# Attention ahead of two feed-forward networks: plain float32 products on quarters and halves of TensorE's array in place of exact float32r halves

## The chip, the cores and the metric

One NeuronCore of one Trainium2 chip runs the whole program. The metric is the device time of one execution in microseconds; lower is better. A difference is judged by the median of several executions of both kernels on the same chip.

## What is computed

Attention over a sliding window of 64 positions, for 4 batches, 8 heads, 576 positions and a head size of 64. Its result, as 2304 rows of 512, goes through two networks: first the elementwise maximum of three products and an output product, then a product, a clipped square and another product.

```python
scores = np.matmul(q, k.transpose(0, 1, 3, 2)) / np.sqrt(64)
mask = (rel >= 0) & (rel < 64)                 # rel = query position - key position
attn = softmax(np.where(mask, scores, -1e9))   # sum + 1e-9 below the fraction
x = np.matmul(attn, v).transpose(0, 2, 1, 3).reshape(2304, 512)
h = np.maximum(np.maximum(x @ w1, x @ w2), x @ w3)   # w: 512 x 768
y = h @ w_out                                        # 768 x 512
h2 = y @ w_in                                        # 512 x 2048
g = np.where(h2 >= 1, h2, np.where(h2 <= -1, 0, (h2 + 1) ** 2 / 4))
out = g @ w_out2                                     # 2048 x 512
```

q, k and v are float32; the six weights are float64 in memory, 512 KB per tile.

## The kernel before

**Groups.** The 2304 positions are 36 groups of 64 positions, each with all 8 heads, as 4 pairs of heads: on the 128 partitions lie two heads of a pair, or 64 queries of each. Every group sees a window of 128 keys, its own 64 and the 64 ahead (64 keys for a batch's first group). Four groups make one block of 256 rows for the first network, of which there are nine.

**Exact halves.** A float32r product takes its operands at reduced precision. So the kernel splits each operand into a rounded high part and the rest (`sub` computes the rest), and adds three products, high by high, high by rest, rest by high. Weights, network inputs and, in this kernel, all attention operands are treated so. The networks stay as they are in the change.

**Stages of a group.** Each stage is a function, and the diff touches most of them:

- `load` and `vload` bring q, k and v. For the first 16 groups (`PET`) q and k come in natural layout, two groups on 128 partitions (`nat`); for later ones in pieces for VectorE's transposition (`raw`). v comes as keys by heads (`vr`).
- `prep` transposes q and k, for the first 16 groups on TensorE (`tp`, L234; one group is one half of the rows of `nat`), and writes q's halves, scaled, into a block-diagonal tile (`qbd`, ScalarE and L251) and k's halves into a ring of four groups (`kring`).
- `vprep` splits v (`vhl`, VectorE's L264 and a GpSimd subtraction).
- `qk` makes the scores `sps` (L287, L288; two products per pair), adds high and low parts and the mask (`t`, L292), then the negated scores and their minimum (`sm`, `nm`, L295).
- `ex` is the exponential (L306), `norm` the division (GpSimd, L317).
- `ptr` transposes the weights on TensorE (`pps`, L326) and splits them (`pthl`).
- `pv` multiplies them with v (`ops`, L339, L342; again two products per pair), adds the two parts (`xs`, `x`, L350) and splits the result into the network's input `xt`.

In what follows a score visit is a group's run of `sps` products on TensorE, a value visit its run of `ops` products.

**Weights.** `w_load` and `w_split` bring a float64 tile (`wst`) and turn it into a high and a rest part in `u`: three ScalarE operations, two VectorE ones (L156, L157), one on GpSimd. Four buffers hold tiles that wait for this. The first network has 24 such tiles, the second 32.

**Order.** The stages of the first four groups stand in an order written out by hand (`SEQ`). Those of the later ones get a due time by `STAGES`, relative to the items of the first network (`a_item`, L369, and `b_item`, L391). All is sorted by due time; then the framework's scheduler, which works with costs of its own, sets the order on each engine. Each engine runs its queue in order. All loads go through SyncE's queue.

**Buffers in PSUM.** `tp` and the networks' `ps` share three tiles of one bank (`pmm`); `sps` takes two banks, `pps` one, `ops` two.

## Time and profile before

| | us |
|---|---|
| median of 3 runs (875.35 to 876.76) | 876.25 |
| the profiled execution | 875.89 |
| its span, first to last instruction | 873.8 |
| TensorE busy with matmuls | 827.7 (95%) |
| VectorE busy | 497.1 (57%) |
| ScalarE busy | 419.9 (48%) |
| GpSimd busy | 202.0 (23%) |

Between the profiled execution's own time and its span lie 2.1 us of start and end. Rows of a timeline give the start, the duration, the engine, the line, the operation, the tiles it writes and reads, the used rows by columns of the array for a matmul, and how many merge in the row. Rows of a stretch give each engine's busy time with its number of instructions, the clock granted to TensorE (PEclk), the share of the DMA engines and GB/s. Rows of groups give the busy time, the mean duration in ns, and the idle time ahead.

### The profile page before, as it was taken

The page shows a single profiled execution, that of the slowest core. Times are in us where ns is not written, and L with a number is a line of the kernel's source. Part 1 is how long each engine was busy: PE and PEld are TensorE (multiplying, and loading weights), DVE is VectorE, ACT ScalarE, POOL GpSimd, SP SyncE. Part 2 cuts the span into 40 slices and gives each one's busy share as a digit, 9 for nine tenths or more (in the row PEclk, how much of TensorE's full clock was granted, in tenths as well). Part 3 has the DMA queues.
Part 4 walks back from the last instruction along what each step waited for, and adds up shares of the span by engine and source line. Part 5 has one row for each costly group of instructions (what it writes and reads, how often), then busy time and mean ns, then how long its engine had stood idle before and what let it go on. Part 6 is the DMA issues. An engine that isn't in the chain of part 4 may idle for free.

```text
span 873.8 us, 14317 instructions
## 1 busy us (share of the span) xinstructions
PE 827.7 (95%) x5264; PEld 743.7 (85%) x5264; DVE 497.1 (57%) x1216; ACT 419.9 (48%) x1043; POOL 202.0 (23%) x194
## 2 busy tenths in 40 slices
PE   5667899999999999999988999999999999999998
PEld 4567899999999999999877888888888888888897
DVE  5899975685858566645777833533343333333343
ACT  6997745564646475644778522322232223222232
POOL 3565642332323223333565300000000000000000
PEclk9998999999999999999999999999999999999999
DMA  9864534223414321202767100200010000100000
GB/s 235 195 167 145 153 65 89 65 52 66 80 45 72 109 62 43 79 20 68 229 222 248 60 1 1 74 11 1 1 48 25 1 1 12 49 1 1 24 25 25
DMA packets 128053, 62.66 MB, mean 72 GB/s; under 512 B 98288, under 2 KB 120816, under 8 KB 127984
## 3 DMA queue, kind: packets, MB, share of 16 engines
q1 hardware_dynamic: 127984, 61.76, 26.7%
q8 instruction: 41, 0.67, 0.3%
q14 instruction: 28, 0.23, 0.1%
HBM read 52.30 MB, written 9.44 MB: 71 GB/s over the span
## 4 chain that ended last, share of the span: by engine, by line
PE 79%; DVE 9%; DMA 5%; ACT 3%; issue 3%; POOL 1%; SPq 0%; DVEq 0%; ACTq 0%; POOLq 0%
PE acc L577 23%; PE hp L528 23%; PE ps L369 19%; PE ps L391 6%; DMA wst<-in_moe_w_in 3%; PE ops L339 2%; PE sps L287 2%; DVE wt L157 2%; DVE wt L156 2%; PE pps L326 1%; DMA wst<-in_moe_w_out 1%; POOL u L100 1%; PE sps L288 1%; PE ops L342 1%; DVE t L292 1%
## 5 line engine op out<-in xcount | busy, mean ns | idle before, releaser
L369 PE MATMUL ps<-xt,u 128*128 128x256 f32 x1944 | 246.7, 283 | 9.7 <-DVE ht L378 3.9
L369 PEld LDWEIGHTS ps<-xt,u 128*128 128x128 f32 x1944 | 235.1, 190 | 12.6 <-DVE ht L378 4.9
L557 ACT ACTIVATE u<-hp,half 128x512 f32<-128x512 f32 (+1 forms) x80 | 51.6, 645 | 253.8 <-PE hp L528 253.8
L528 PE MATMUL hp<-x2t,u 128*128 128x512 f32 (+1 forms) x720 | 161.6, 372 | 0.0
L577 PE MATMUL acc<-u,g 128*128 128x512 f32 x648 | 160.4, 396 | 0.0
L528 PEld LDWEIGHTS hp<-x2t,u 128*128 128x128 f32 x720 | 126.9, 188 | 27.2
L560 DVE SCALAR_TENSOR_TENSOR gt<-u,hp 128x512 f32<-128x512 f32 (+1 forms) x80 | 50.6, 632 | 166.7 <-ACT u L558 166.6
L577 PEld LDWEIGHTS acc<-u,g 128*128 128x128 f32 x648 | 121.0, 188 | 28.3
L391 PE MATMUL ps<-h,u 128*128 128x256 f32 x648 | 82.4, 284 | 4.6 <-ACT x2s L97 2.9
L391 PEld LDWEIGHTS ps<-h,u 128*128 128x128 f32 x648 | 78.5, 190 | 5.7 <-ACT x2s L97 3.1
L100 POOL TENSOR_TENSOR u<-wt,u 128x512 fp32r<-128x512 f32 x48 | 66.0, 1378 | 40.9 <-ACT u L97 40.8
L306 ACT ACTIVATE sm<-sm,nm 128x128 f32<-128x128 f32 (+1 forms) x144 | 55.3, 386 | 20.2 <-DVE nm L295 19.8
L317 POOL TENSOR_TENSOR sm<-sm,rs 128x512 f32<-128x512 f32 (+1 forms) x36 | 36.3, 1008 | 121.0 <-DVE rs L316 61.8
L564 DVE CAST g<-gt 128x512 fp32r<-128x512 f32 (+1 forms) x80 | 35.0, 437 | 45.6 <-PE acc L577 43.0
L100 POOL TENSOR_TENSOR vhl<-vr,vhl 128x512 fp32r<-128x512 f32 (+1 forms) x35 | 46.1, 1317 | 58.8 <-DVE vhl L264 24.8
L100 POOL TENSOR_TENSOR h<-ht,h 128x256 fp32r<-128x256 f32 x54 | 41.7, 773 | 65.2 <-ACT h L97 65.1
L157 DVE CUSTOM_DVE_ANT_0 wt<-wst,wt 128x1024 uint16<-128x1024 uint16 x56 | 54.2, 970 | 1.0
L528 PE MATMUL hp<-x2t,v 128*128 128x512 f32 (+1 forms) x240 | 54.4, 375 | 0.1
L287 PE MATMUL sps<-kring,qbd 128*128 128x256 f32 (+1 forms) x144 | 44.4, 377 | 10.4 <-DVE nm L295 8.4
L577 PE MATMUL acc<-v,g 128*128 128x512 f32 x216 | 53.6, 394 | 0.0
L100 DVE TENSOR_TENSOR g<-gt,g 128x512 fp32r<-128x512 f32 (+1 forms) x80 | 51.1, 639 | 2.6
L378 DVE TENSOR_TENSOR ht<-ps,ht 128x256 f32<-128x256 f32 x108 | 45.1, 418 | 10.6 <-PE ps L369 8.1
(68 smaller groups left out, 1067.2 us busy)
## 6 DMA issues: line engine op xcount, KB each, us to landing
wst<-in_moe_w_out SPq DMA_DIRECT2D x22, 512.0 KB, 4.3
wst<-in_moe_w SPq DMA_DIRECT2D x18, 512.0 KB, 4.1
wst<-in_moe_w_in SPq DMA_DIRECT2D x16, 512.0 KB, 4.1
vr<-in_v SPq DMA_DIRECT2D x24, 256.0 KB, 3.5
x_scratch<-x2s SPq DMA_DIRECT2D x36, 128.0 KB, 1.8
out<-ob SPq DMA_DIRECT2D x18, 256.0 KB, 2.0
x2r<-x_scratch SPq DMA_DIRECT2D x16, 256.0 KB, 2.8
vr<-in_v SPq DMA_DIRECT2D x19, 128.0 KB, 3.2
```

Source lines behind the costliest of these rows:

```text
L100: eng.tensor_tensor(dst, a, b, op=ALU.subtract)
L157: nc.vector.tensor_tensor(t, t, lo, op=ALU.add)
L287: nc.tensor.matmul(o[:, 0:2 * W], qh(p), win(p, slice(0, 2)), start=True, stop=False)
L306: nc.scalar.activation(sm[:, p, 0:W], sm[:, p, 0:W], AF.Exp, bias=d["nm"][:, p:p + 1], scale=-1.0, accum_out=ss[:, p:p + 1])
L317: nc.gpsimd.tensor_tensor(sm[:, :, 0:W], sm[:, :, 0:W], rs.unsqueeze(2).to_broadcast([P, NP, W]), op=ALU.mult)
L369: nc.tensor.matmul(ps[:, 0:n], w_col((w, f), wl, kt), xt[:, xl, kt, 0:n], start=(x == 0), stop=(x == len(passes) - 1))
L378: nc.vector.tensor_tensor(t[:, 0:n], ps[:, 0:n], part[j, f][:, 0:n], op=ALU.max)
L391: nc.tensor.matmul(ps[:, 0:n], w_col((3, f), wl, dt), hts[j, f][:, xl, 0:n], start=(x == 0), stop=(x == len(passes) - 1))
L528: nc.tensor.matmul(ps[:, 0:n], w_col((4, f), wl, kt), x2t[tb][:, xl, kt, 0:n], start=(x == 0), stop=(x == len(passes) - 1),)
L557: nc.scalar.activation(u[:, 0:n], ps[:, 0:n], AF.Relu, bias=half, scale=2.0 ** (-WS / 2 - 1))
L560: nc.vector.scalar_tensor_tensor(gt[:, 0:n], u[:, 0:n], 2.0 ** WS, ps[:, 0:n], op0=ALU.min, op1=ALU.max)
L577: nc.tensor.matmul(accs[t], g[:, gl, t * P:(t + 1) * P], wslot[5, f][:, wl * 512:(wl + 1) * 512], start=(f == 0 and x == 0), stop=(f == KF ...
```

## The change

The attention's operands are no longer split. Scores and values are plain float32 products.

- `prep`: for the first 16 groups, q and k of two groups are transposed at once, on the full array (L237), q copied to `qt2` by ScalarE, k to the ring by VectorE (L242). Later groups are transposed by VectorE straight to `qt` and the ring.
- `vprep` is gone; `pv` reads `vr`.
- `qk`: each head of a pair is a product of 64 rows by 64 columns of the array, the first head's on the upper left quarter, the second's on the lower right one (L272). `sps` is one bank, with two buffers. The scale of q has moved into L275, which now adds the mask itself.
- `ptr`: one copy in place of copy and rest.
- `pv`: each head is a product of its own on one half of the array's columns (L318), whose results lie where the network's input wants them; no sum of parts follows.
- `vr` has four buffers for two, `sm`, `nm`, `ss` and `rs` three for two. The hand order and the list of due times lose the entries of the stages that are gone.

```diff
-    "L0 V1 P0 P1 L2 V2 V3 v1 Q0 Q1 E0 N0 E1 N1 P2 T0 P3 Q2 v2 X0 T1 Q3 E2 N2 v3 E3 X1 N3 "
+    "L0 V1 P0 L2 V2 V3 Q0 Q1 E0 N0 E1 N1 P2 T0 Q2 X0 T1 Q3 E2 N2 E3 X1 N3 "
...
-    kring = apool.tile([P, NP, 2, 4, BL], F32R, name="kring")
-    qbd = [apool.tile([P, 2, NP, 2, BL], F32R, name=f"qbd{i}") for i in range(2)]
+    kring = apool.tile([P, NP, 4, BL], F32, name="kring")
...
     def prep(g):
         if g in pet:
-            tp = pmm.tile([P, 2, NP, BL], F32, tag="mm", name="tp")
-            r = slice(g % 2 * BL, g % 2 * BL + BL)
+            if g % 2:
+                return
+            qt = apool.tile([P, NP, 2, BL], F32, tag="qt2", name="qt2", bufs=2)
             for x in range(2):
+                tp = pmm.tile([P, NP, P], F32, tag="mm", name="tp")
                 for p in range(NP):
-                    nc.tensor.transpose(tp[:, x, p, :], nat[g // 2][r, x, p * P:(p + 1) * P], ident[r, r])
-            qt, kt = tp[:, 0], tp[:, 1]
+                    nc.tensor.transpose(tp[:, p, :], nat[g // 2][:, x, p * P:(p + 1) * P], ident)
+                tp = tp.rearrange("a p (t c) -> a p t c", t=2)
+                if x == 0:
+                    act_copy(qt, tp)
+                else:
+                    nc.vector.tensor_copy(kring[:, :, s:s + 2, :], tp)
...
-        qb = qbd[g % 2]
-        for h in range(2):
-            r = slice(h * BL, h * BL + BL)
-            act_copy(qb[r, 0, :, h, :], qt[r], scale=QSCALE)
-        act_copy(kring[:, :, 0, s, :], kt)
-        for h in range(2):
-            r = slice(h * BL, h * BL + BL)
-            nc.vector.scalar_tensor_tensor(
-                qb[r, 1, :, h, :], qt[r], QSCALE, f32(qb[r, 0, :, h, :]), op0=ALU.mult, op1=ALU.subtract
-            )
-        sub(nc.vector, kring[:, :, 1, s, :], kt, f32(kring[:, :, 0, s, :]))
...
     def qk(g):
-        sps = patt.tile([P, NP, 2, 2 * BL], F32, tag="s", name="sps")
+        sps = patt.tile([P, NP, 2 * BL], F32, tag="s", name="sps", bufs=2)
         for p in range(NP):
-            o = sps[:, p].rearrange("a b c -> a (b c)")
-            nc.tensor.matmul(o[:, 0:2 * W], qh(p), win(p, slice(0, 2)), start=True, stop=False)
-            nc.tensor.matmul(o[:, 0:W], ql(p), win(p, 0), start=False, stop=True)
-        t = apool.tile([P, NP, 2 * BL], F32, tag="t", name="t", bufs=1)
-        mb = mask.unsqueeze(1).to_broadcast([P, NP, W])
-        nc.vector.tensor_tensor(t[:, :, 0:W], sps[:, :, W:2 * W], mb, op=ALU.add)
+            for h in range(2):
+                r = slice(h * BL, h * BL + BL)
+                nc.tensor.matmul(sps[r, p, 0:W], d["q"][r, p, :], win(r, p), start=True, stop=True)
...
-                out=sm[:, p, 0:W], in0=sps[:, p, 0:W], in1=t[:, p, 0:W], scale=-1.0, scalar=BIG,
+                out=sm[:, p, 0:W], in0=sps[:, p, 0:W], in1=mask, scale=-QSCALE, scalar=BIG,
...
     def ptr(g):
-        act_copy(pt[0:W, :, 0, :], pps[0:W])
-        sub(nc.vector, pt[0:W, :, 1, :], pps[0:W], f32(pt[0:W, :, 0, :]))
+        act_copy(pt[0:W], pps[0:W])
...
     def pv(g, xt, off):
-        ops = patt.tile([P, NP, 2, P], F32, tag="o", name="ops")
+        ops = patt.tile([P, NP, BL], F32, tag="o", name="ops")
         for p in range(NP):
-            o = ops[:, p].rearrange("a b c -> a (b c)")
-            vc = slice(p * P, (p + 1) * P)
-            nc.tensor.matmul(
-                o, vh[0:W, 0, vc], pt[0:W, p].rearrange("a b c -> a (b c)"), start=True, stop=False
-            )
-            nc.tensor.matmul(o[:, 0:P], vh[0:W, 1, vc], pt[0:W, p, 0, :], start=False, stop=True)
-        for h in range(2):
-            r = slice(h * BL, h * BL + BL)
-            act_copy(xs[r], ops[r, :, 1, r])
-        for h in range(2):
-            r = slice(h * BL, h * BL + BL)
-            nc.vector.tensor_tensor(x[r], ops[r, :, 0, r], xs[r], op=ALU.add)
-        act_copy(xt[:, 0, :, off:off + BL], x)
-        sub(nc.vector, xt[:, 1, :, off:off + BL], x, f32(xt[:, 0, :, off:off + BL]))
+            for h in range(2):
+                r = slice(h * BL, h * BL + BL)
+                nc.tensor.matmul(ops[r, p, :], vr[0:W, 2 * p + h, :], pt[0:W, p, r], start=True, stop=True)
+        act_copy(xt[:, 0, :, off:off + BL], ops)
+        sub(nc.vector, xt[:, 1, :, off:off + BL], ops, f32(xt[:, 0, :, off:off + BL]))
```

**How it moves the order.** A row of an order is a line, an operation, the tile written and the tiles read, the shape, and how many follow each other. On TensorE, the start of the program before; the tiles are numbered here, `tp_133` being group 0, on the upper half of the rows, `tp_148` group 1, on the lower half, `tp_225` group 2:

```order
L234 MATMUL tp_133<-ident_85,nat_128 128x64 x4
L234 MATMUL tp_148<-ident_85,nat_128 128x64 x4
L234 MATMUL tp_133<-ident_85,nat_128 128x64 x4
L234 MATMUL tp_148<-ident_85,nat_128 128x64 x4
L234 MATMUL tp_225<-ident_85,nat_163 128x64 x4
```

And the start after, without numbers:

```order
L237 MATMUL tp<-ident,nat 128x128 x8
L272 MATMUL sps<-kring,qt_129 64x64 x8
L272 MATMUL sps<-kring,qt_129 64x128 x8
L237 MATMUL tp<-ident,nat 128x128 x8
L306 MATMUL pps<-ident,sm 64x128 x4
```

Sixteen transpositions on halves of the rows have become eight on the full array, and the scores of both groups follow each other.

On VectorE, the work from the first transpositions to the first scores before:

```order
L264 CAST vhl<-vr 128x512
L251 SCALAR_TENSOR_TENSOR qbd_102<-tp,qbd_102 64x4x64 x2
L100 TENSOR_TENSOR kring<-tp,kring 128x4x64
L251 SCALAR_TENSOR_TENSOR qbd_103<-tp,qbd_103 64x4x64 x2
L100 TENSOR_TENSOR kring<-tp,kring 128x4x64
L292 TENSOR_TENSOR t<-sps,maskA 128x4x64
L295 ISA sm,nm<-sps,t 128x64
```

And after:

```order
L242 COPY kring<-tp 128x4x128
L275 ISA sm,nm<-sps,maskA 128x64
```

One copy for two groups stands where eight operations stood ahead of the first scores' reduction.

On TensorE among the first network's products, a score visit before:

```order
L369 MATMUL ps<-xt,u_66 128x256 x12
L287 MATMUL sps<-kring,qbd_102 128x256
L288 MATMUL sps<-kring,qbd_102 128x128
L287 MATMUL sps<-kring,qbd_102 128x256
L288 MATMUL sps<-kring,qbd_102 128x128
L287 MATMUL sps<-kring,qbd_102 128x256
L288 MATMUL sps<-kring,qbd_102 128x128
L287 MATMUL sps<-kring,qbd_102 128x256
L288 MATMUL sps<-kring,qbd_102 128x128
L369 MATMUL ps<-xt,u_67 128x256 x12
```

And after, a score visit and a value visit:

```order
L337 MATMUL ps<-xt,u_70 128x256 x12
L272 MATMUL sps<-kring,qt_1095 64x128 x8
L337 MATMUL ps<-xt,u_71 128x256 x12
L318 MATMUL ops<-pt,vr 64x64 x8
L337 MATMUL ps<-xt,u_72 128x256 x12
```

Eight products on quarters or on halves stand where eight on the full array stood, between the same neighbours; they come and go by a change of the array's shape.

More of the change, by code (lines that the diff above doesn't have):

```diff
@@ L38 @@
 TAIL = 15
-STAGES = (-21, -9, -3, -2.5, 0, 0.2, 1, 6, 9)
+STAGES = (-21, -9, -3, 0, 0.2, 1, 6, 9)
 LP = -9
@@ L215, in vload @@
             return
-        t = apool.tile([P, H, D], F32, tag="vr", name="vr", bufs=2)
+        t = apool.tile([P, H, D], F32, tag="vr", name="vr", bufs=4)
         if i == 0:
@@ L243, in prep @@
                 )
-        qb = qbd[g % 2]
-        for h in range(2):
-            r = slice(h * BL, h * BL + BL)
-            act_copy(qb[r, 0, :, h, :], qt[r], scale=QSCALE)
-        act_copy(kring[:, :, 0, s, :], kt)
-        for h in range(2):
-            r = slice(h * BL, h * BL + BL)
-            nc.vector.scalar_tensor_tensor(
-                qb[r, 1, :, h, :], qt[r], QSCALE, f32(qb[r, 0, :, h, :]), op0=ALU.mult, op1=ALU.subtract
-            )
-        sub(nc.vector, kring[:, :, 1, s, :], kt, f32(kring[:, :, 0, s, :]))
-    def vprep(g):
-        b, i, s = blk(g)
-        d = st_g[g]
-        if g == 0:
-            return
-        n = BL if i == 0 else P
-        vh = apool.tile([P, 2, DM], F32R, tag="vhl", name="vhl", bufs=2)
-        src = d["vr"].rearrange("p h d -> p (h d)")
-        nc.vector.tensor_copy(vh[0:n, 0, :], src[0:n])
-        sub(nc.gpsimd, vh[0:n, 1, :], src[0:n], f32(vh[0:n, 0, :]))
-        d["vhl"] = vh
+            d["q"] = qt
     def window(g):
@@ L271, in window @@
         if i == 0:
-            return lambda p, hl: kring[:, p, hl, s, :], maskA[:, BL:2 * BL], BL
+            return lambda r, p: kring[r, p, s, :], maskA[:, BL:2 * BL], BL
         if natural(g):
-            return lambda p, hl: kring[:, p, hl, s - 1:s + 1, :], maskA, 2 * BL
-        return lambda p, hl: kring[:, p, hl, 0::3, :], maskB, 2 * BL
+            return lambda r, p: kring[r, p, s - 1:s + 1, :], maskA, 2 * BL
+        return lambda r, p: kring[r, p, 0::3, :], maskB, 2 * BL
     def qk(g):
@@ L303, in ex @@
         W, sm = d["W"], d["sm"]
-        ss = apool.tile([P, NP], F32, tag="ss", name="ss", bufs=2)
+        ss = apool.tile([P, NP], F32, tag="ss", name="ss", bufs=3)
         for p in range(NP):
@@ L313, in norm @@
         W, sm, ss = d["W"], d["sm"], d["ss"]
-        rs = apool.tile([P, NP], F32, tag="rs", name="rs", bufs=2)
+        rs = apool.tile([P, NP], F32, tag="rs", name="rs", bufs=3)
         nc.vector.tensor_scalar(ss, ss, EPS, None, op0=ALU.add)
@@ L326, in ptr @@
             nc.tensor.transpose(pps[0:W, p, :], sm[:, p, 0:W], ident)
-        pt = apool.tile([P, NP, 2, P], F32R, tag="pthl", name="pthl", bufs=2)
-        act_copy(pt[0:W, :, 0, :], pps[0:W])
-        sub(nc.vector, pt[0:W, :, 1, :], pps[0:W], f32(pt[0:W, :, 0, :]))
+        pt = apool.tile([P, NP, P], F32, tag="pt", name="pt", bufs=2)
+        act_copy(pt[0:W], pps[0:W])
         d["pt"] = pt
@@ L413 @@
     nc.scalar.activation(half, half, AF.Exp, scale=0.0)
-    nc.gpsimd.memset(f32(qbd[0]), 0.0)
-    nc.gpsimd.memset(f32(qbd[1]), 0.0)
     make_identity(nc, ident)
@@ L445 @@
     order = []
-    stages = (load, vload, prep, vprep, qk, ex, norm, ptr, pv_x)
+    stages = (load, vload, prep, qk, ex, norm, ptr, pv_x)
     def put(at, fn, *args):
@@ L487 @@
         at += cost
[L490 removed]
+    ops0 = dict(L=load, V=vload, P=prep, Q=qk, E=ex, N=norm, T=ptr, X=pv_x)
     for x, tok in enumerate(SEQ.split()):
```

19 lines of the change are left out of this document (7 added, 12 removed).

## The prediction

> **What bounds the kernel now.** I read the page's span first, then the busy time by stretch, then the early part of the chain of waits, the groups of the first 60 us, and the timeline of TensorE where the changed products stand.
>
> ```profile
> span 873.8 us, 14317 instructions
> core 0: us, PE busy (x) PEld busy (x) DVE busy (x) ACT busy (x) POOL busy (x), PEclk, DMA share, GB/s
> 0.00:20.00 20.00, 10.59 (x68) 8.87 (x68) 10.95 (x43) 12.08 (x35) 6.56 (x16) 1.00 1.12 237
> 20.00:60.00 40.00, 26.13 (x125) 23.75 (x126) 37.50 (x116) 36.33 (x103) 22.30 (x19) 1.00 0.78 191
> 60.00:100.00 40.00, 33.43 (x254) 32.32 (x253) 38.49 (x77) 31.18 (x79) 25.24 (x22) 0.91 0.56 165
> 100.00:400.00 300.00, 296.72 (x2543) 294.26 (x2542) 199.20 (x633) 170.65 (x529) 97.08 (x99) 1.00 0.28 64
> ```
>
> Two regimes stand here. From 20 to 100 us VectorE is busy 37.50 and 38.49 of each 40 us and TensorE is not. From 100 to 400 us TensorE is busy 296.72 of 300. Nearly all attention work lies in these two stretches; the last value products end just behind the second, and the second network after them is not touched. So the change is priced twice: by what it takes from VectorE before 100 us, and by what TensorE pays for a group after. The chain up to 75 us agrees, with VectorE's lines in front:
>
> ```profile
> by line: issue 14.9%; DVE wt L157 12.6%; DVE wt L156 10.2%; DVE t L292 6.5%; ACT sm L306 6.0%; DMA nat<-in_k 5.4%; DVE sm L295 5.2%; DVE x L350 5.0%; DVE pthl L100 4.2%; DVE qbd L251 4.2%; DVE kring L100 2.7%; DVE vhl L264 2.6%; DVE xt L100
> ```
>
> **Lead-in, part by part.** VectorE's groups in the first 60 us, then ScalarE's that change and one whose price I need:
>
> ```profile
> L157 DVE CUSTOM_DVE_ANT_0 wt<-wst,wt 128x1024 uint16<-128x1024 uint16 x11 | 9.6, 872 | 0.0
> ...
> L251 DVE SCALAR_TENSOR_TENSOR qbd<-tp,qbd 64x256 fp32r<-64x256 f32 x16 | 6.6, 415 | 0.6 <-ACT kring L97 0.4
> ...
> L292 DVE TENSOR_TENSOR t<-sps,maskA 128x512 f32<-128x512 f32 (+1 forms) x7 | 4.5, 646 | 0.9 <-PE sps L288 0.9
> L264 DVE CAST vhl<-vr 128x512 fp32r<-128x512 f32 x5 | 4.0, 793 | 2.2 <-DMA vr<-in_v 2.2
> L100 DVE TENSOR_TENSOR pthl<-pps,pthl 128x512 fp32r<-128x512 f32 (+1 forms) x5 | 3.4, 684 | 0.1
> L100 DVE TENSOR_TENSOR kring<-tp,kring 128x256 fp32r<-128x256 f32 x8 | 3.4, 424 | 0.1
> L350 DVE TENSOR_TENSOR x<-ops,xs 64x256 f32<-64x256 f32 x8 | 3.3, 418 | 0.1
> ```
> ```profile
> L97 ACT ACTIVATE qbd<-tp 64x256 fp32r<-64x256 f32 x16 | 6.0, 373 | 4.1 <-PE tp L234 3.9
> L97 ACT ACTIVATE kring<-tp 128x256 fp32r<-128x256 f32 x8 | 3.1, 383 | 0.2
> L97 ACT ACTIVATE xs<-ops 64x256 f32<-64x256 f32 x8 | 3.0, 371 | 0.0
> L97 ACT ACTIVATE pthl<-pps 128x512 fp32r<-128x512 f32 (+1 forms) x5 | 2.9, 590 | 0.1
> ```
>
> The exact halves of q, k, v, of the transposed weights and of the two-part result go, and with them six VectorE groups: 6.6 + 4.5 + 4.0 + 3.4 + 3.4 + 3.3 = 25.2 us of VectorE's 48.5 (10.95 + 37.50). Added are four copies of a pair's k from PSUM, 128x512; nearest row 684 ns, 2.7 us. VectorE falls to some 26 us. ScalarE loses 6.0 + 3.1 + 3.0 = 12.1 of 48.4 and gains four copies of q at 590 ns, 2.4, so it keeps about 39; in the new order eight split weights, not ten, stand ahead of the first feed-forward product, which leaves some 36. GpSimd loses its subtraction for v, which is not late there (22.30 of 40). TensorE in this part:
>
> ```profile
> 5.35 0.70 PE L234 MATMUL tp<-ident,nat 64*128 64x64 f32 x8 [0.43 <-DMA nat<-in_k]
> 7.74 0.69 PE L234 MATMUL tp<-ident,nat 64*128 64x64 f32 x4 [1.69 <-DMA nat<-in_q]
> ...
> 25.18 1.11 PE L234 MATMUL tp<-ident,nat 64*128 64x64 f32 x8
> ...
> 41.82 1.08 PE L326 MATMUL pps<-ident,sm 128*128 128x128 f32 x4
> 59.70 5.16 PE L369 MATMUL ps<-xt,u 128*128 128x256 f32 x36
> ```
>
> The first feed-forward product starts at 59.70. Until then TensorE runs at about half of its later pace, though PEclk reads 1.00 (four transpositions end after 1.08 here, after 0.60 below): 128 float32 columns at 0.11 us below are some 0.21 here. The new program has ahead of that product 8 score visits, 4 value visits, 6 transpositions of weights and 32 of q and k: 8 x 1.7 + 4 x 1.3 + 6 x 0.85 + 32 x 0.21 = 31 us of TensorE (the visits at twice the prices below), from 5.35 on. So no engine has more than 36 us where VectorE had 48. With 6 us before the first data comes, 42 is the floor, 52 about as far as waits in the chain of eight groups may push it; I take 46, a gain of 14. Between 60 and 100 us TensorE is idle 6.6 us and loses 3.6 to the clock (PEclk 0.91 of 40); VectorE sheds there the same groups for two to four visits. Of these 10 I take 4, since the weights' own splitting stays. Lead-in: -18, bounds -9 and -25.
>
> **Steady part, per visit.** TensorE is full here, so each nanosecond counts.
>
> ```profile
> 157.53 0.60 PE L326 MATMUL pps<-ident,sm 128*128 128x128 f32 x4
> 157.88 1.66 PE L369 MATMUL ps<-xt,u 128*128 128x256 f32 x12
> 159.38 0.28 PE L287 MATMUL sps<-kring,qbd 128*128 128x256 f32 x1
> ...
> 160.24 3.02 PE L369 MATMUL ps<-xt,u 128*128 128x256 f32 x24
> 163.10 2.26 PE L391 MATMUL ps<-h,u 128*128 128x256 f32 x18
> 165.20 0.28 PE L339 MATMUL ops<-pthl,vhl 128*128 128x256 f32 x1
> ...
> 166.15 0.71 PE L234 MATMUL tp<-ident,nat 64*128 64x64 f32 x8
> 166.79 4.47 PE L391 MATMUL ps<-h,u 128*128 128x256 f32 x36
> ```
> ```profile
> 213.93 0.60 PE L326 MATMUL pps<-ident,sm 128*64 128x128 f32 x4
> 214.28 0.36 PE L287 MATMUL sps<-kring,qbd 128*128 128x256 f32 x1
> ```
>
> A score visit takes 160.24 - 159.38 = 0.86 us. A value visit has the same shapes, yet 166.15 - 165.20 = 0.95: the 0.09 more is the change to products on half of the rows. Eight of these then take 0.64 up to the next product, less two changes 0.46, 0.058 each. Four float32 products of 128 columns take 0.35, and the twelve behind them 1.50 where 18 x 0.117 (163.10 to 165.20) gives 1.41: 0.44, or 0.11 each.
>
> *Scores.* Eight products become, as the program is built, sixteen matmul instructions (5,776 instructions in all, for 5,184 products, against 5,264), each over 128 float32 columns: 16 x 0.11 = 1.75 us one after another, 0.87 if the two quarters run side by side. No row of before has quarters. The nearest are transpositions on halves of the rows: at 5.35 four on the upper and four on the lower half take 0.70, as long as four on one half at 7.74 (0.69), while eight on one half at 25.18 take 1.11. Two halves of the rows do run side by side. I take 0.87: 28 visits, +0.3 us; the bounds are 0.44 (one instruction at this price) and 1.75, -12 to +25.
>
> *Values.* Sixteen instructions over 64 columns: 0.93 one after another at 0.058, 0.46 side by side. Here the halves are of columns and share their rows; no row shows such overlap. I take the middle, 0.65: 32 x (0.65 - 0.86) = -6.7, bounds -13 and +2.
>
> *Changes of shape.* After the first feed-forward product the new order has 70 changes between products on half of the rows and others, the old one 22: 48 x 0.09 = +4.3. The half-column shape seems free: four at 213.93 take 0.35 like the full form at 157.53. The Trainium skill says (TensorEngine Tiling (Array Packing), Key Properties) that changing the tiling mode, not just the tile, drains the engine. The trace agrees for halves of rows, with 0.09 us, and not for halves of columns; by the page the 53 more changes of that kind would add 4.8 us and the sum would end near 861.
>
> *Transposing q and k for two groups.* 32 x 0.11 for 64 x 0.058: -0.2.
>
> Steady: +0.3 - 6.7 + 4.3 - 0.2 = -2.3. The other removals (VectorE, ScalarE, GpSimd after 100 us) I cost at nothing: TensorE covers them, VectorE being busy 199 of 300. No DMA is added. A buffer of v now comes free at its value products instead of at GpSimd's subtraction, which is later, and there are four instead of two; behind those loads SyncE's queue holds the weights' loads, which so wait no longer than before. Sum: 873.8 + 2.1 around the span = 875.9 (the profiled execution, 0.4 below the median of 876.25), less 18, less 2.3: 856.
>
> **The rivals.**
> *The quarters run one after another.* Both quarters of a group's scores go to one PSUM bank, `sps` being 2 KB per partition, while the transpositions that overlap at 5.35 go to two tiles. Then a visit costs 1.75: 28 x 0.88 = +25; and in the lead-in TensorE has 8 x 1.7 = 14 us more, 45 from 5.35 on, so it starts at 52 or later and the gain there shrinks by about 8. 856 + 25 + 8 = 889, slower than before. It decides from a visit of about 1.5 us on. Against it: the quarters write different partitions. The Trainium skill (the same page, Gotcha 1: PSUM Pressure) says that different row tiles cannot access the same PSUM bank simultaneously, which is this case; no row here shows two row halves writing one bank.
> *The column halves don't overlap.* Values at 0.93: +9 us, 865. For it: they share their rows. Against it: nothing but the free change at 213.93.
> *The lead-in hardly shortens.* Transfers were at a share of 1.12 in the first 20 us and 0.78 in the next 40, and ScalarE at 36.33 of 40; if the chain of exponentials and weights sets the pace, the first product comes at 54 and the sum is 866.
>
> **How the numbers follow.** The forecast has 0.50, quarters one after another 0.20, column halves 0.18, the lead-in 0.12. The likeliest gives 856. Its bounds of lead-in (+9, -7) and values (+9, -6) together make 842 to 874; the two milder rivals lie inside. To leave out no more than 2 in 10, the top goes to 884, towards the first rival, whose lower end (values side by side) is 883. A change within 0.2% (1.75 us) is about what can't be told from none. Faster: nearly all of the forecast and the milder rivals, 0.75; same 0.05; slower: the first rival and a little, 0.20.
>
> **What would show it.** Right: VectorE no longer full between 20 and 60 us, the first feed-forward product near 46, score visits near 0.87 plus two changes, value visits near 0.65, TensorE full from 100 us on. Wrong: score visits of 1.75 and starts of the second quarter behind the end of the first; a first product after 54; gaps at shape changes well over 0.09; or TensorE waiting on ScalarE, now the busiest, between 40 and 100 us.

## The result, and the profile after

The changed kernel takes 848.69 us (median of 4 runs, 847.96 to 849.46), beside 875.8 for the kernel before: a ratio of 0.9692 with an interval of 0.9675 to 0.9709, or 27.1 us less. The profiled execution has a span of 847.3 us. The forecast of 856 had the sign right and the lead-in as the main place, and was 7 us too high.

Busy time by stretch, the changed kernel (same columns as before: TensorE, its weight loads, VectorE, ScalarE, GpSimd, granted clock, share of the DMA engines, GB/s):

```profile
span 847.3 us, 14830 instructions
0.00:20.00 20.00, 11.43 (x108) 9.02 (x108) 9.51 (x42) 12.77 (x39) 5.41 (x15) 0.94 1.09 235
20.00:60.00 40.00, 33.17 (x347) 29.71 (x347) 31.01 (x98) 36.06 (x103) 23.34 (x20) 0.86 1.08 259
60.00:100.00 40.00, 38.21 (x364) 35.86 (x364) 28.84 (x72) 29.20 (x76) 24.10 (x21) 1.00 0.55 142
100.00:380.00 280.00, 280.00 (x2769) 267.00 (x2768) 91.47 (x389) 114.90 (x366) 55.90 (x66) 1.00 0.29 65
```

From 20 to 60 us TensorE is busy 33.17 where it was 26.13, and VectorE 31.01 where it was 37.50. ScalarE still has 36.06, and the transfers rose from 191 to 259 GB/s. From 100 us on TensorE is full. Its rows at the first product of the first network and at the changed visits:

```profile
27.71 0.60 PE L306 MATMUL pps<-ident,sm 128*128 128x128 f32 x4
28.24 0.69 PE L318 MATMUL ops<-pt,vr 128*64 128x64 f32 x16
29.00 1.96 PE L272 MATMUL sps<-kring,qt 64*64 64x128 f32 x32
...
37.74 4.51 PE L337 MATMUL ps<-xt,u 128*128 128x256 f32 x22
...
108.06 1.09 PE L272 MATMUL sps<-kring,qt 64*64 64x128 f32 x16
109.08 2.37 PE L359 MATMUL ps<-h,u 128*128 128x256 f32 x18
111.29 1.56 PE L337 MATMUL ps<-xt,u 128*128 128x256 f32 x12
112.78 0.69 PE L318 MATMUL ops<-pt,vr 128*64 128x64 f32 x16
113.39 4.47 PE L337 MATMUL ps<-xt,u 128*128 128x256 f32 x36
```

The first feed-forward product starts at 37.74, not 59.70. A score visit takes 109.08 - 108.06 = 1.02 us up to the next product, a value visit 113.39 - 112.78 = 0.61. Sixteen instructions of 0.11 us in 1.02 are two quarters side by side. Before them there is a gap of 0.20 from the last product's start, where 0.12 was usual.

Three places, then, by the start of the same feed-forward product in both traces (product N of the first network, counted from 0; the last row is the second network's 25th first product):

| | before | after | difference |
|---|---|---|---|
| product 0 | 59.70 | 37.74 | -22.0 |
| product 187 | 100.23 | 71.72 | -28.5 |
| product 400 | 135.17 | 106.34 | -28.8 |
| product 2200 | 407.34 | 376.91 | -30.4 |
| second network | 472.69 | 446.12 | -26.6 |

The lead-in gives 28.5 us, the steady part about 2, and the passage to the second network takes 3.9 back. What TensorE spends between products 300 and 2200, from each instruction's start to the next one's start, summed by what it computes (us):

| | before | after | difference |
|---|---|---|---|
| scores | 23.24 | 24.70 | +1.5 |
| values | 23.72 | 15.98 | -7.7 |
| transposing the weights (mostly ahead of scores) | 8.68 | 13.00 | +4.3 |
| feed-forward products (these stand ahead of values) | 228.56 | 230.54 | +2.0 |
| transposing q and k | 2.55 | 1.80 | -0.8 |
| all | 286.75 | 286.03 | -0.7 |

In TensorE's busy time these products cost 1.1 us more than before (286.0 for 284.9); the -0.7 comes from 1.8 us of idle time that only the kernel before has there. The +2.0 is a change of shape: the last product ahead of values lasts 0.21 us where 0.12 is usual, 26 times 0.09. In the +4.3 stands one visit more (26 for 25), and the last transposition ahead of scores, which lasts 0.20 us now and 0.03 before, 22 times. Of these 0.17, 0.09 are the change of shape, since with scores on the full array (an experiment below) 0.11 is left. At the passage, from product 2200 to the 25th of the second network, the rows of before and of after:

```profile
407.34:472.69 65.35, 56.32 (x419) 52.48 (x417) 47.84 (x67) 47.83 (x95) 38.96 (x33) 0.97 0.70 222
```
```profile
376.91:446.12 69.21, 58.12 (x418) 53.61 (x417) 51.95 (x72) 51.62 (x101) 43.28 (x34) 0.95 0.70 218
```

The same products take 3.9 us longer: 1.8 of it busy time (the clock, 0.95 for 0.97: half speed for 6.8 us, not 3.4), and 2.1 idle (69.21 - 58.12 = 11.1 against 9.0). TensorE's longest waits there, before and after (us in total, times, longest):

```profile
PE ps L369 <- ACT x2s L97: 3.0, 3, 1.5
PE ps L391 <- ACT x2s L97: 2.9, 1, 2.9
PE ps L391 <- ACT ht L97: 1.4, 2, 1.1
```
```profile
PE ps L359 <- ACT x2s L99: 3.6, 2, 3.1
PE ps L337 <- ACT ht L99: 2.8, 3, 1.3
PE ps L337 <- ACT x2s L99: 2.3, 3, 1.8
```

Each names ScalarE, which waits there itself for the weights of the second network, before and after:

```profile
ACT wst L152 <- DMA wst<-in_moe_w_in: 6.5, 9, 1.4
ACT wst L152 <- DMA wst<-in_moe_w_out: 5.2, 7, 1.9
```
```profile
ACT wst L153 <- DMA wst<-in_moe_w_in: 10.2, 11, 1.7
ACT wst L153 <- DMA wst<-in_moe_w_out: 1.1, 3, 0.5
```

That wait did not grow: 11.7 us in sum before, 11.3 after. Nor do the weights lag behind the first network: their first load in this stretch is issued at 410.93 before and at 379.00 after, 3.6 and 2.1 us behind product 2200. Why TensorE idles 2.1 us longer stays open, and part of it may be chance of the two executions profiled: the kernels of the experiments, which have the same two networks, take 66.5 to 70.3 us over these products.

### The profile page after: what moved, and what is told of

Read it like the earlier page. It is cut to its first block, busy times and chain, and to the rows that moved or that the text cites. A ratio compares the mean times of both kernels' runs of the same rounds, so it can differ in the third digit from the quotient of the medians.

```text
span 847.3 us, 14830 instructions
## 1 busy us (share of the span) xinstructions
PE 815.0 (96%) x5776; PEld 716.9 (85%) x5776; DVE 366.4 (43%) x937; ACT 357.9 (42%) x871; POOL 158.9 (19%) x157
## 4 chain that ended last, share of the span: by engine, by line
PE 84%; DVE 4%; DMA 4%; ACT 3%; issue 2%; POOL 1%; DVEq 0%; SPq 0%; ACTq 0%; POOLq 0%
PE acc L543 24%; PE hp L494 24%; PE ps L337 21%; PE ps L359 8%; PE sps L272 4%; PE ops L318 2%; DVE wt L157 2%; DVE wt L158 2%; DMA wst<-in_moe_w_in 1%; PE pps L306 1%; POOL u L102 1%; DMA nat<-in_k 1%; DMA x2r<-x_scratch 1%; ACT wst L153 1%; PE tp L237 1%
## 5 line engine op out<-in xcount | busy, mean ns | idle before, releaser
L102 POOL TENSOR_TENSOR u<-wt,u 128x512 fp32r<-128x512 f32 x48 | 68.7, 1436 | 42.1 <-ACT u L99 40.4
L99 ACT ACTIVATE h<-ht 128x256 fp32r<-128x256 f32 x54 | 22.4, 415 | 78.3 <-DVE ht L346 78.3
L157 DVE TENSOR_SCALAR wt<-wst 128x512 int32<-128x512 int32 x56 | 43.1, 770 | 26.2 <-POOL u L102 14.3
L530 DVE CAST g<-gt 128x512 fp32r<-128x512 f32 (+1 forms) x80 | 33.1, 414 | 45.8 <-PE acc L543 43.7
```

The costliest lines, as they stand in the source:

```text
L102: eng.tensor_tensor(dst, a, b, op=ALU.subtract)
L157: nc.vector.tensor_scalar(t, hi, 3, None, op0=ALU.logical_shift_left)
```

## The experiments

All times are medians with the ratio to the kernel before, measured beside them (875.09, 875.61 or 875.86). "Against the changed kernel" is the difference of the ratios to 0.9692, times 875.

### How the quarters share the array

**Runs of eight instructions.** The loop over the two heads is put outside the loop over the pairs, in scores and in values:

```diff
-        for p in range(NP):
-            for h in range(2):
+        for h in range(2):
+            for p in range(NP):
```

> The changed kernel, with the products of a visit in another order: all four pairs of the first head (one quarter or half of the array), then all four of the second. Theory: the two quarters, and the two column halves, run side by side by themselves, as the transpositions on two row halves did in the trace of before though four and four followed each other. Then a score visit stays at 1.02 us up to the next product and a value visit at 0.62, and the time at 848 to 850 us. Rival: products start in program order, and only their alternation lets them overlap. Then the score visit takes 16 x 0.107 + 0.15 = 1.9 and the value visit 16 x 0.055 + 0.15 = 1.0, the time goes up by 27 x 0.88 + 31 x 0.4 = 36 us to about 885.

Measured: 872.85 us, ratio 0.9969 [0.9951, 0.9987], 24 us above the changed kernel. A score visit and the product behind it:

```profile
112.00 1.58 PE L272 MATMUL sps<-kring,qt 64*64 64x128 f32 x16
113.51 1.21 PE L359 MATMUL ps<-h,u 128*128 128x256 f32 x8
```

A visit takes 1.51 us, between side by side (1.02) and one after another (about 1.9). So both answers were too simple. The single records inside this row tell how. They do not name the quarter, but their starts fall into two even streams of eight, each with 0.11 us from one instruction to the next, and I read each stream as one quarter. The second quarter's first instruction starts at 112.497, together with the first quarter's fifth (112.491) and ahead of its sixth (112.600). So four instructions of each stream overlap and the other four run alone: by this reading TensorE starts work on another quarter ahead of the program's order, but only from some four instructions ahead. Values behave alike, 0.90 us in place of 0.61.

**Runs of four instructions.** That reading says how short a run must be, so it was tried:

```diff
-        for p in range(NP):
-            for h in range(2):
+        for p, h in ((0, 0), (1, 0), (0, 1), (1, 1), (2, 0), (3, 0), (2, 1), (3, 1)):
```

> The changed kernel with the products of scores and values in runs of two on one quarter or half (four instructions), then two on the other, where the changed kernel alternates after each one (two instructions) and the kernel with runs of four (eight instructions) took 1.51 for a score visit. Theory (TensorE takes up an instruction only some four places ahead of the one that runs: with runs of eight the second quarter's first started together with the first quarter's fifth): runs of four still overlap fully, a score visit 1.02 to 1.05, a value visit 0.62 to 0.65, time 848 to 850. Rival (overlap falls off evenly with the length of the run): a visit near 1.2, a value visit near 0.7, time 855 to 858.

Measured: 852.22 us, ratio 0.9738 [0.9722, 0.9755], 4 us above the changed kernel.

```profile
110.14 1.14 PE L271 MATMUL sps<-kring,qt 64*64 64x128 f32 x16
111.21 2.38 PE L357 MATMUL ps<-h,u 128*128 128x256 f32 x18
113.42 1.56 PE L335 MATMUL ps<-xt,u 128*128 128x256 f32 x12
114.92 0.73 PE L316 MATMUL ops<-pt,vr 128*64 128x64 f32 x16
115.58 0.61 PE L335 MATMUL ps<-xt,u 128*128 128x256 f32 x3
```

1.07 and 0.66 us: each visit is half an instruction longer, since from the sixth pair on the two quarters run half a step apart. A drop that is even in the run's length would have given 1.2. The reading stands; the visits are up to 0.02 above the theory's range, and the time is 2 us above it (58 visits by 0.05 = 2.9 us, and 1.6 in the lead-in).

**Scores on the full array.** The two heads' q in one block-diagonal float32 tile, one product for a pair, eight instructions a visit, no change of shape:

```diff
-            for h in range(2):
-                r = slice(h * BL, h * BL + BL)
-                nc.tensor.matmul(sps[r, p, 0:W], d["q"][r, p, :], win(r, p), start=True, stop=True)
+            nc.tensor.matmul(
+                sps[:, p, 0:W], qbd[g % 4][:, p].rearrange("a b c -> a (b c)"), win(p), start=True, stop=True
+            )
```

> The changed kernel, with the scores as plain float32 products on the full array: q block-diagonal with zeros, four products of 128 rows by 128 columns per group in place of eight on quarters. The same passes (8 matmul instructions of 128 float32 columns, 0.11 each, 0.88 us), but no change of the array's shape. Theory: a change costs 0.09 on entry and 0.15 on the way out, so a visit falls from 0.09 + 1.02 to 0.88, over some 27 visits 6 us; ScalarE has four copies of 64x256 (1.5 us) where it had one of 128x512 (0.6) per two groups in the lead-in, which may cost 1 to 2: 843 to 845 us. Rival: the gaps at the edges of a visit are no cost of the shape (the full array shows them too): 849 to 851 us.

Measured: 844.57 us, ratio 0.9643 [0.9624, 0.9661], 4 us below the changed kernel.

```profile
110.99 1.05 PE L275 MATMUL sps<-kring,qbd 128*128 128x128 f32 x8
111.80 2.35 PE L364 MATMUL ps<-h,u 128*128 128x256 f32 x18
```

A visit takes 0.81 for 1.02, and the row ahead loses its drain. Between products 300 and 2200 scores cost 19.49 us for 24.70 and the transpositions ahead of them 11.01 for 13.00: together 7.2 less. Of this about 1 us is one visit that lies outside these products in this form (24 for 25); a visit of the full window is 0.30 cheaper, 0.21 by itself and 0.09 ahead of it. Product 0 starts at 39.97, though, 2.2 later; ScalarE copies q four times for a pair of groups there, not once (the last kernel below tests this).

**Values on the full array.** One product for a pair of heads, of which half the result is read:

```diff
-            for h in range(2):
-                r = slice(h * BL, h * BL + BL)
-                nc.tensor.matmul(ops[r, p, :], vr[0:W, 2 * p + h, :], pt[0:W, p, r], start=True, stop=True)
+            nc.tensor.matmul(
+                ops[:, p, :], vr[0:W, 2 * p:2 * p + 2, :].rearrange("a b c -> a (b c)"), pt[0:W, p, :],
+                start=True, stop=True,
+            )
```

> The changed kernel, with the values as plain float32 products on the full array: four products of 128 by 128 columns per group in place of eight on column halves, half of each result unused; two copies and two subtractions of 64 partitions take the result out. 8 instructions of 0.11 us, 0.88, against 0.615 + 0.09 now. Theory: the column halves run side by side and that outweighs two changes of shape: +0.17 x 31 = 5 us, 853 to 855. Rival: the halves hardly overlap and the visit's 0.46 is something else, or the changes cost as much as the overlap brings: 848 to 850.

Measured: 855.2 us, ratio 0.976 [0.974, 0.9781], 6 us above the changed kernel. A visit takes 117.52 - 116.71 = 0.81:

```profile
116.71 1.05 PE L316 MATMUL ops<-pt,vr 128*128 128x128 f32 x8
117.52 2.70 PE L342 MATMUL ps<-xt,u 128*128 128x256 f32 x21
```

Less the 0.09 ahead of the column halves, the split gains 0.11 a visit, and the products 300 to 2200 take 2.5 us longer here (288.5 for 286.0). The larger part of the 6 us has another place: product 300 already starts 4.8 us later. This form also takes its result out in two copies and two subtractions of 64 partitions, not shown above, and up to there they cost ScalarE 7.5 us for 3.7 and VectorE 8.4 for 4.1; that they make the 4.8 is likely, but was not tested apart.

So for values the split pays, for scores it does not. The reason is in the counts: a head's scores need the full 128 columns of the window in either form, so two quarters side by side take as long as one full product (0.87 against 0.81) and pay two drains besides; a head's values need 64 columns instead of 128, so two halves side by side take about half of it (0.46), and the drains leave a gain.

### Where the lead-in's 28 us come from

**VectorE's work put back, dead.** As many VectorE operations, of the sizes that the change removed, whose results are not read, in the first 8 groups:

```diff
+                    if g < 8:
+                        for y in range(6):
+                            dead(tp[:, :, y % 2, :])
...
+        if g < 8:
+            dead(sps[:, :, 0:W])
...
+        if 1 <= g < 8:
+            dead(pps)
+            dead(d["vr"])
...
+        if g < 8:
+            dead(ops)
+            dead(ops)
```

> The changed kernel with VectorE work put back in the first eight groups: subtractions of zero with unused results, in the sizes and at the places of the work that the change removed (six of 128x256 per pair of groups at the transposition, one of 128x512 at the scores, two of 128x512 at the transposed weights, two of 128x256 at the values), some 25 us in all. Theory: VectorE bounded the lead-in, so the first feed-forward product goes from 37.7 back to 52 to 58 us, and the time by 14 to 20 us to 863 to 869. Rival: the lead-in is shorter for ScalarE's relief, TensorE's shorter chain or the new order; then the product stays before 42 and the time below 853.

Measured: 869.66 us, ratio 0.9929 [0.9906, 0.9951], 21 us above, where 14 to 20 were expected. The first product came at 41.07 and not behind 52, so that part of the expectation failed, though it stands behind six score visits there and not eight. The dead operations took 32.4 us up to product 187, more than the 25 expected. Product 400 starts at 127.98, 21.6 later than in the changed kernel: the cost falls between 41 and 95 us.

```profile
20.00:60.00 40.00, 25.85 (x219) 22.60 (x220) 37.35 (x101) 30.63 (x79) 17.68 (x14) 0.70 0.88 219
60.00:100.00 40.00, 30.28 (x296) 26.58 (x295) 36.20 (x87) 30.79 (x82) 25.24 (x21) 0.87 0.56 154
```

**ScalarE's work, dead.** The same with ScalarE, 32 copies of 128x256:

```diff
+                    if g < 8:
+                        for y in range(4):
+                            dead(tp[:, :, y % 2, :])
...
+        if g < 8:
+            dead(ops)
+            dead(ops)
```

> The changed kernel with dead ScalarE copies of 128x256 elements in the first 8 groups (4 at each pair's q, 2 at each value visit; some 32 x 0.38 = 12 us of ScalarE, nothing else changed). Theory (with VectorE lightened, ScalarE at 36 of 40 us and the transfers set the lead-in, so it has no slack): the time goes up by 8 to 12 us, 857 to 861. Rival (the chain of each group, not any engine, sets it, and ScalarE has slack): up by at most 3, 849 to 852.

Measured: 871.83 us, ratio 0.9953 [0.9933, 0.9972], 23 us above: twice the theory's upper end. Product 400 starts at 129.98, 23.6 later.

```profile
L99 ACT ACTIVATE dead<-tp 128x256 f32<-128x256 f32 x16 | 6.0, 378 | 0.1
L99 ACT ACTIVATE dead<-ops 128x256 f32<-128x256 f32 x16 | 6.0, 376 | 0.0
```
```profile
20.00:60.00 40.00, 20.64 (x174) 16.36 (x175) 27.83 (x82) 36.81 (x102) 21.42 (x18) 0.66 0.91 234
60.00:100.00 40.00, 35.25 (x309) 32.76 (x309) 21.49 (x57) 28.47 (x75) 19.49 (x17) 0.87 0.57 143
```

12.0 us of ScalarE cost 24, where 32.4 of VectorE cost 22. There was no slack on ScalarE, so the rival is out. What comes with the doubled price shows in the second pair of rows: the granted clock is 0.66 and 0.87 where the changed kernel has 0.86 and 1.00, or (0.20 + 0.13) x 40 = 13 us of full-speed time less, which counts where TensorE has work; and VectorE, which had nothing added, waits. Its wait for GpSimd (which itself waits for ScalarE's split weights) is 13.8 us up to product 187, where it was 3.0:

```profile
L157 DVE TENSOR_SCALAR wt<-wst 128x512 int32<-128x512 int32 x24 | 15.7, 656 | 15.4 <-POOL u L102 13.8 <-ACT wst L153 1.7
```

So the lead-in is set by no single engine but by the chain through ScalarE, VectorE and GpSimd, whose queues are in order. How the extra 12 us divide between clock and chain was not separated. The dead operations also read `tp`, `sps`, `pps` and `ops` and so keep these tiles in use for longer; what part of either price that is was not separated either.

**Values alone.** The kernel before with the change's value part: no halves of v and of the transposed weights, one product a head, no sum of parts, four buffers for v.

```diff
-            nc.tensor.matmul(
-                o, vh[0:W, 0, vc], pt[0:W, p].rearrange("a b c -> a (b c)"), start=True, stop=False
-            )
-            nc.tensor.matmul(o[:, 0:P], vh[0:W, 1, vc], pt[0:W, p, 0, :], start=False, stop=True)
+            for h in range(2):
+                r = slice(h * BL, h * BL + BL)
+                nc.tensor.matmul(ops[r, p, :], vr[0:W, 2 * p + h, :], pt[0:W, p, r], start=True, stop=True)
```

> The kernel before with the change's values part alone: v and the transposed weights not split, one float32 product for each head on half of the array's columns; scores and q and k as before. Theory (each part pays where its own rows stand): steady, 32 visits at 0.70 (0.615 and 0.09 on entry) for 0.86 give -5; in the lead-in VectorE loses v's, the weights' and the result's groups, 4.0 + 3.4 + 3.3 of its 25.2 us, so some 40% of the 28 us, -8 to -14. Sum -13 to -19 against the kernel before: 856 to 862. Rival (the lead-in's gain comes whole or not at all, since VectorE stays the fullest): -5 to -8, 867 to 870.

**Scores alone.** The kernel before with the other part: quarters, q and k for two groups; v, the weights and values as before.

```diff
-            nc.tensor.matmul(o[:, 0:2 * W], qh(p), win(p, slice(0, 2)), start=True, stop=False)
-            nc.tensor.matmul(o[:, 0:W], ql(p), win(p, 0), start=False, stop=True)
+            for h in range(2):
+                r = slice(h * BL, h * BL + BL)
+                nc.tensor.matmul(sps[r, p, 0:W], d["q"][r, p, :], win(r, p), start=True, stop=True)
```

> The kernel before with the change's q, k and scores part alone: quarters, q and k transposed for two groups; v, the transposed weights and values as before. Theory: steady, 27 visits at 1.11 for 0.86 give +7; in the lead-in VectorE loses 6.6 + 4.5 + 3.4 of 25.2 us, some 60% of the 28, -14 to -20. Sum -7 to -13 against the kernel before: 862 to 868. Rival (VectorE was by far the bound, and half of what it loses already moves the bound to ScalarE and the transfers): lead-in -24 or more, sum -17, 858.

Measured: values alone 850.15 us, ratio 0.9707 [0.969, 0.9723]; scores alone 870.75, ratio 0.9943 [0.9928, 0.9958]. Neither the theory nor the rival of either was met; both had the split the wrong way round. Against the kernel before, values alone are worth 25.6 us, scores alone 5.0. By stage:

| start of | values alone | scores alone | sum | both (the change) |
|---|---|---|---|---|
| product 0 | -15.3 | -5.2 | -20.5 | -22.0 |
| product 187 | -19.1 | -9.3 | -28.4 | -28.5 |
| product 2200 | -28.0 | -6.5 | -34.5 | -30.4 |
| second network | -25.8 | -5.2 | -31.0 | -26.6 |

In the lead-in the parts add up to the whole. From product 187 to 2200 they do not: -8.9 and +2.7 against -1.9. Of the 4.3 us between, 2.5 are idle time of TensorE, 3.3 us there before and 0.5, 2.1 and 1.8 in these three kernels, so both parts take some of the same idle time away. But values, with 10.7 of the 25.2 us that VectorE loses, give two thirds of the lead-in's gain. VectorE's and ScalarE's time by stretch, values alone and then scores alone:

```profile
20.00:60.00 40.00, 33.27 (x248) 29.43 (x248) 35.38 (x109) 36.30 (x109) 23.34 (x19) 1.00 0.86 211
```
```profile
20.00:60.00 40.00, 23.32 (x145) 20.39 (x146) 34.48 (x90) 35.89 (x97) 27.07 (x21) 0.59 0.88 222
```

VectorE and ScalarE are nearly equally busy in both, and yet the first network is 10 us further in the first. The clock does not explain it: the 1.00 of the first row is no measurement up to 51.9 us, where the trace's first record of the clock stands, and four transpositions take 1.12 us at 35.59, half pace. At half pace up to 51.9 us the stretch would have some 0.60, an estimate, like the second row. Busy time on the fullest engine doesn't tell which step is worth taking away. So each step of the value part was put back by itself, for the first 9 groups.

**Result step put back.** Into the changed kernel, for the first 9 groups, the copy and the two-operand step between value products and the network's input (a maximum of two equal numbers, so nothing else changes):

```diff
+        if g < HOP:
...
+            for h in range(2):
+                r = slice(h * BL, h * BL + BL)
+                act_copy(xs[r], ops[r])
+            for h in range(2):
+                r = slice(h * BL, h * BL + BL)
+                nc.vector.tensor_tensor(x[r], ops[r], xs[r], op=ALU.max)
+            ops = x
```

> The changed kernel with the step of before between value products and the network's input put back for the first 9 groups, in the chain: two ScalarE copies of 64x256 and two VectorE operations on two operands of 64x256 (a maximum, so the values stay). Theory (what a step costs in the lead-in goes by its time on VectorE and ScalarE together; the three steps of values, 12.7, 6.2 and 7.0 us of them up to product 187, are worth the 19 that the kernel with the values part alone gained there): +9 to +11, 858 to 860. Rival (GpSimd's part of v's split is most of the 19): at most +4, 853.

**Weights' second step put back.** VectorE's step between ScalarE's copy of the transposed weights and the products:

```diff
+        if g < HOP:
+            p1 = apool.tile([P, NP, P], F32, tag="p1", name="p1", bufs=2)
+            nc.vector.tensor_tensor(p1[0:W], pps[0:W], pt[0:W], op=ALU.max)
+            pt = p1
```

> The changed kernel with the second step of before for the transposed weights put back for the first 9 groups, in the chain: one VectorE operation on two operands of 128x512 (a maximum, so the values stay) between ScalarE's copy and the value products. Theory (price by time on VectorE and ScalarE, 6.2 us of 25.9 for 19): +4 to +6, 853 to 855. Rival (GpSimd's part of v's split is most of the 19): at most +3, 852.

**v's steps put back.** VectorE's and GpSimd's, ahead of the value products:

```diff
+        nc.vector.tensor_scalar(v0[0:W], vr[0:W], 0.0, None, op0=ALU.mult)
+        nc.gpsimd.tensor_tensor(v1[0:W], vr[0:W], v0[0:W], op=ALU.add)
+        d["vr"] = v1
```

> The changed kernel with the two steps of before for v put back for the first 9 groups, in the chain and at their old places in the order: a VectorE operation on 128x512 (times zero) and a GpSimd addition of 128x512, whose result the value products read. Theory (price by time on VectorE and ScalarE, 7.0 us of 25.9 for 19; GpSimd, busy 37 of 72 us, has slack): +5 to +6, 854 to 855. Rival (GpSimd's 12 us stand in its queue ahead of the normalizing products and of the split weights, and are most of the 19): +10 or more, 859 or more.

Measured: result step 857.16 us, ratio 0.9792 [0.9767, 0.9816]; weights' step 855.06, 0.9772 [0.9755, 0.9789]; v's steps 850.8, 0.9721 [0.9704, 0.9739]. Against the changed kernel +8.7, +7.0 and +2.5 us. Product 400 starts 8.8, 7.4 and 2.5 later: 18.7 together, close to the 21.4 that values alone gain there. The interval of v's steps still touches the changed kernel's (0.9704 and 0.9709). What was put back, in the same order (groups of the first 80 us), and under the result step the subtraction behind it, which now reads `x`:

```profile
L328 DVE TENSOR_TENSOR x<-ops,xs 64x256 f32<-64x256 f32 x16 | 6.7, 418 | 0.1
L103 DVE TENSOR_TENSOR xt<-x,xt 128x256 fp32r<-128x256 f32 x8 | 7.9, 992 | 0.0
```
```profile
L100 ACT ACTIVATE xs<-ops 64x256 f32<-64x256 f32 x16 | 6.0, 374 | 0.1
```
```profile
L312 DVE TENSOR_TENSOR p<-pps,pt 128x512 f32<-128x512 f32 (+1 forms) x9 | 6.1, 680 | 0.1
```
```profile
L236 DVE TENSOR_SCALAR v<-vr 128x512 f32<-128x512 f32 x8 | 5.8, 726 | 1.9 <-POOL v L237 1.9
```
```profile
L237 POOL TENSOR_TENSOR v<-vr,v 128x512 f32<-128x512 f32 x8 | 10.9, 1364 | 8.0 <-DVE v L236 5.8 <-issue 1.0 <-POOL sm L310 1.0
```

The weights' step and v's have nearly the same time on VectorE (6.1 and 5.8 us) and cost 7.0 and 2.5. The weights' step stands in a group's chain from weights to network input, between two engines; v's stand off it, since v is loaded early, and most of the 10.9 us on GpSimd is hidden. The result step, 8.7, stands in the chain too but is no like for like: beside its 6.7 us on VectorE it has 6.0 on ScalarE, and the subtraction behind it takes 992 ns in place of 416, 4.6 us more for eight. The theory (price by engine time) was slightly too high for the result step (857.16, 858 to 860 expected), too low for the weights' step and too high for v; the rival on GpSimd is out.

The price need not be the chain's alone. From 20 to 60 us the granted clock is 0.69, 0.74 and 0.80 in these three kernels and 0.86 in the changed one: 6.8, 4.8 and 2.4 us less of full-speed time, in the same order as the prices. How much of a price is the step's own delay and how much the lower clock that came with it is not separated.

### A version that takes both gains

Quarters for the first 8 groups, scores on the full array for the others:

```diff
+            for h in range(2 if g < QTR else 0):
+                r = slice(h * BL, h * BL + BL)
+                nc.tensor.matmul(sps[r, p, 0:W], d["q"][r, p, :], win(p, r), start=True, stop=True)
+            if g < QTR:
+                continue
+            nc.tensor.matmul(
+                sps[:, p, 0:W], qbd[g % 4][:, p].rearrange("a b c -> a (b c)"), win(p), start=True, stop=True
+            )
```

> The kernel with scores on the full array (844.57), but its first 8 groups, which stand in the lead-in, with the changed kernel's quarters and one copy of q for two groups in place of four. Theory (the block form costs 3.5 us in the lead-in by its four small copies of q and gains 8 behind it by 0.29 a visit): both gains together, 844.6 - 3 = 841 to 842, 7 us below the changed kernel. Rival (the 3.5 us come from the first pass of the blocks' clearing or from chance in the clock's half-speed stretches, not from the copies): no change, 844 to 846.

Measured: 840.29 us, ratio 0.9597 [0.958, 0.9615]: 8 us below the changed kernel and 4 below the full form. Product 0 starts at 38.69 (37.74 in the changed kernel, 39.97 in the full form), product 600 at 137.58 (137.47 and 139.52). So the small copies of q account for 1.9 us up to there, not 3.5. Another 1.5 us separate it from the full form at the passage to the second network, where TensorE's clock stayed at 1.00 in this kernel's profiled execution, while the full form's was at half speed for 3.4 us, or 1.7 us lost. That the time came out near the theory's 841 to 842, just below it, is thus in part another cause's doing. The row of the passage, to be held against the changed kernel's above (0.95):

```profile
370.82:437.35 66.53, 55.20 (x418) 51.13 (x417) 50.25 (x71) 49.69 (x98) 41.95 (x33) 1.00 0.71 221
```

## Why the prediction was right, and where it missed

**The lead-in was named rightly and sized too low.** Forecast -18 with an outer bound of -25; it is -28.5, of which the first product's start gives 22.0 (forecast 14) and the stretch behind it 6.5 (forecast 4). The step that failed is the floor: "eight split weights, not ten, stand ahead of the first feed-forward product, which leaves some 36", and from that 42 as the earliest start. Six stood ahead, and ScalarE had 29.4 us of work in 37.7:

```profile
0.00:37.74 37.74, 23.45 (x248) 18.95 (x248) 23.46 (x104) 29.38 (x95) 14.52 (x23) 0.87 1.09 236
```

Also, TensorE was costed at half pace throughout, 31 us. The rows at 27.71 and 28.24 above are at full pace (0.60 for four transpositions, not 1.08): the granted clock was full from 24.4 to 34.6 us. And the argument that VectorE loses 25.2 of its 48.5 us took the fullest engine for the bound. The runs showed a chain through three engines instead: dead work on VectorE or on ScalarE each takes 21 us or more back, and steps of 6.1 and 5.8 us on VectorE cost 7.0 in the chain and 2.5 off it.

**Scores.** Forecast 0.87 a visit plus two changes, a sum of +0.3; the visit is 0.87 and 0.15 to the next product, and the kind cost +1.5 from product 300 to 2200 (25 of the 28 visits). The rival that the quarters run one after another, 889 us, did not come about. (The products number 5,200 by the trace's instructions, not 5,184; nothing hangs on it.) The Trainium skill's sentence behind it (TensorEngine Tiling (Array Packing), Gotcha 1: PSUM Pressure, that different row tiles cannot access the same PSUM bank simultaneously) is contradicted here: two row halves write different partitions of one bank, sixteen instructions of 0.11 us in 1.02. But the overlap hangs on the program's order, which no step of the prediction saw: with runs of eight nearly the whole gain is lost, 872.85.

**Values.** Forecast 0.65 as the middle of 0.46 and 0.93; the column halves overlap fully, 0.46 and the gap of 0.15 behind: -7.7 in 26 visits, or 0.30 each, against -6.7 for 32, or 0.21 each.

**Changes of shape.** Forecast +4.3, with the half-column shape taken as free from the transpositions at 213.93. It isn't free: the product ahead of values lasts 0.21 instead of 0.12, like that ahead of the quarters. From product 300 to 2200 the entries to either shape cost some 2 us, and on the way out the next product on the full array starts 0.15 to 0.20 behind the last one, where it is 0.03 behind scores or values on the full array; this part stands in the visits. Here the Trainium skill (same page, Key Properties: changing the tiling mode drains the engine) was right for column halves too, at 0.09 us on entry. The four half-column transpositions that showed nothing were too thin a ground.

**The steady sum.** -0.7 between products 300 and 2200, -1.9 from 187 on, against -2.3 forecast. That these are close is luck: TensorE's busy time, which the forecast priced, rose by 1.1 and fell by 0.4 us, and the rest is idle time of before that went (1.8 and 1.5 us).

**"I cost at nothing"** was said of all other removals after 100 us, TensorE covering them, and nothing was forecast for the second network's start. That missed the idle time just named, and the passage at 377 to 446 us, where the cover is gone and 3.9 us go back: 1.8 of busy time at a lower clock, and 2.1 of idle time whose cause stays open. "TensorE waiting on ScalarE", which the prediction looked for between 40 and 100 us, stands here, before as after.

**The total.** The time lies well within the range, though the lead-in is 3.5 us outside its own bound; the passage, which nobody had priced, takes about as much back.

## What to carry to other kernels

Splitting a product over parts of the array pays where each part then streams fewer columns (values), and not where every part streams as many as the full product did (scores): each change of shape costs about 0.09 us on entry and 0.12 to 0.17 on the way out here, and the two streams must alternate within some four instructions to overlap. Before TensorE is full, price a removed step by its place in the chain between engines, not by the share of the fullest engine; one step put back at a time shows that price, the lower clock that comes with it included. A gain in an early stage need not arrive whole at the end: compare the start of the same product stage by stage.

## What the runs showed of the hardware that was not expected

- TensorE starts an instruction on another quarter ahead of earlier ones of the program, as read from two even streams of starts: in the kernel with runs of eight, the ninth instruction of a visit starts at 112.497, the sixth at 112.600. It reaches only some four instructions ahead (1.51 us a visit for runs of eight, 1.07 for four, 1.02 for two).
- Two row halves of the array write one PSUM bank side by side: 1.02 us for 16 instructions of 0.11.
- A change of shape costs 0.09 us on entry for half columns too (0.205 against 0.118), and a float32 product of 128 columns is two instructions of 0.11 us each.
- A delay in the lead-in comes with a lower clock: 12.0 us of added ScalarE work came with a granted clock of 0.66 in place of 0.86 from 20 to 60 us, and moved the end by 23 us.
- In the trace of before there is no record of the clock ahead of 61.2 us, and with values alone none ahead of 51.9, so the 1.00 up to there is no measurement; four transpositions took 1.08 us at 41.82 in before and 0.60 later.
